# An attention backward kernel: column form instead of row form of V times dO for nine heads

## The chip, the cores and the metric

One core of one Trainium2 chip. The metric is device time in microseconds (us) of one execution. The kernel before takes 1744.86 us, the median of three runs (1738.73, 1744.86 and 1744.99).

## The reference, cut to what matters

The reference is one decode step of a transformer block with cached attention and a gated feed-forward part, and the gradients of its result towards ten of its inputs. There are B = 2 batch entries with H = 32 heads each, so 64 heads; each head has a cache K and a cache V of 8192 rows and 128 columns in bf16 (2 MB each). Per head, with one query row q and the gradient dO of the head's output o:

```python
p  = softmax(q @ K.T * Dh ** -0.5)     # 8192 numbers
o  = p @ V                              # 128 numbers
# backward
dV = outer(p, dO)                       # 8192 x 128, written out
dP = V @ dO                             # 8192 numbers: "V times dO"
dS = p * (dP - sum(o * dO))
dK = outer(dS, q) * Dh ** -0.5          # 8192 x 128, written out
```

Between the heads' forward and backward parts stands the rest of the block: `o` of all heads of a batch entry goes through `A_wo`, a layer norm and the feed-forward part, and the gradient comes back through the same to dO. This is one dependent chain for each batch entry: the first chain (b = 0) and the second chain (b = 1).

## The kernel before

The kernel is laid out in numbered **slots**. A head's forward job ("A") or backward job ("C") takes 8 slots for its transposes, one group of 8 blocks of 128 x 128 in each slot, and trails further work behind. `sC[n]` is the slot in which the backward job of head n begins. Within a slot, each engine runs its work in the order of the `PL_` numbers: EXP, T, X, S, B, MAX, TT, M, FREE, EV, DS, DK, TASK.[...]

Worked out from the code, with 64 heads, 8 groups a head and a chain of 40 slots (first) and 23 slots (second):

| what | slots |
|---|---|
| forward jobs of heads 0 to 38 | 0 to 312 |
| first chain | 272 to 312 |
| backward heads 0 to 24 alternate with forward heads 40 to 63 | 320 to 712 |
| `A_END`, the end of all forward work | 720 |
| backward heads 25 to 31, eight slots each | 712 to 768 |
| second chain | 721 to 744 |
| dO of batch entry 1, two heads for every two slots | 744 to 777 (the last is `t1`) |
| backward heads 62 and 63 (their V is kept from the forward part) | 768 to 784 |
| backward heads 32 to 61, with the weight gradients between them | 784 to the end |

The transposes of a group go to PSUM (`tp`, 3 buffers) and are copied to `kt` (4 buffers, shared with the chain's own transposes):

```python
def transposes(block, dve):
    tp = tps.tile([P, GRP, P], BF16, name="tp", tag="tp")
    for j in range(GRP):
        nc.tensor.transpose(tp[:, j, :], block(j), identb[:])        # L377
    kt = ktp.tile([P, GRP, P], BF16, name="kt", tag="kt")
    if dve:
        nc.vector.tensor_copy(kt[:], tp[:])                          # L380
    else:
        nc.scalar.copy(kt[:], tp[:])                                 # L382
    return kt

def c_t(n, g):                       # slot s + g
    if g == 0:
        if n in crow:
            nc.gpsimd.tensor_copy(qz[2 + n % 2][...], DO_bf[...])    # L1133
        else:
            DP[n] = head_ps()        # a PSUM bank of the two-buffer pool s_ps
    spare = A_END <= now[0] < t1 or now[0] >= max(sC) - 5 * NG
    kts[("c", n, g)] = transposes(..., g in (2, 6) and not spare)
    ...                              # after half of the groups: V's buffer is released
```

V times dO then has two forms. The **column form** takes each transposed block as weights and dO as one moving column, and leaves the result as a 128 x 64 tile; the **row form** takes dO (padded with zeros) as weights of 32 columns and streams four transposed blocks at once, in four column strips of the array, every second slot; its 128 x 512 result is copied by ScalarE and turned into columns by four fp32 matmuls (eight instructions in the trace):

```python
def c_s(n, g):                       # slot s + g + 2
    if n in crow:
        return s_rows(("c", n), n, g, c_bank)
    kt = kts.pop(("c", n, g))
    for j in range(GRP):             # column form, 8 x 8 = 64 a head
        nc.tensor.matmul(DP[n][:, cc:cc + 1], kt[:, j, :], DO_bf[:, b, h:h + 1], ...)   # L1164

def s_rows(key, i, g, bank):         # row form
    if g % SG < SG - 1:              # SG = 2: only after every second group
        return
    ...
    for j in range(NST):             # 4 x 4 = 16 a head
        nc.tensor.matmul(R_ps[key][NR * j:NR * (j + 1), :], w, kt[:, o:o + SW, :], ...)  # L410
    for k in range(SG):
        kts.pop(kt_of(g - k))

def rows_out(key):                   # slot s + 10
    nc.scalar.copy(t[:], R_ps.pop(key)[:])                           # L417, srow
def cols_out(ps, t):                 # slot s + 11, into a new head_ps()
    for c in range(SW):
        nc.tensor.matmul(sv[:, c, :], t[:, c * P:(c + 1) * P], ssel[:], ...)             # L430
```

The same helper serves the forward scores (L439 is their column form). dV and dK are made by VectorE (L1187) and sent from GpSimd (L1192, 1 MB each); their buffers `half` (21, of which weights and other data hold many during the chain) are the ones that V is loaded into (L187):

```python
x = 1 if n in crow else 0
at(s + 2 * q, PL_TT, ... c_dv(n, q))                        # q = 0..3
at(s + NG + LAG + 1 + (n in crow) + 2 * q, PL_DK, ... c_dk(n, q))
at(s + NG + LAG + x, PL_DS, ... c_ds(n))                    # dS from DP[n], L1208
```

The second chain's small results also lie in `s_ps`: `scr(n)` hands out columns 256 to 511 of the bank that `head_ps()` gave last, while a head uses columns 0 to 63.

Of the kernel before, what the change touches and what calls it, by code (L numbers as in the profile page):

```python
# [17 lines left out]
def kernel(  # L18
# [39 lines left out]
    NHD = B * H  # L58
# [4 lines left out]
    NG = KK // GRP  # L63
# [514 lines left out]
    def end_a(s):  # L578
        return s + MOFF + NG
# [462 lines left out]
    def lay(steps, slot):  # L1042
        for n, f in steps:
            at(slot, PL_TASK, f)
            slot += n
        return slot
# [15 lines left out]
    sC = []  # L1062
# [16 lines left out]
    R0 = min([sA[i] for i in byrows], default=sA[NHD - 1])  # L1079
    A_END = end_a(sA[NHD - 1]) + 1  # L1080
# [5 lines left out]
    t1 = lay(ch[1], CS1)  # L1086
# [53 lines left out]
            release()  # L1140
            pump()

    crow = {n for n in range(NHD) if R0 < sC[n] < max(sC) - 4 * NG}

    def c_bank():
        if now[0] <= A_END:
# [379 lines left out]
```

## Time and profile before

| | before |
|---|---|
| median of three runs | 1744.86 us |
| profiled span | 1742.8 us |
| PE (TensorE matmul) busy | 1454.8 us, 83% |
| DVE (VectorE) busy | 1150.7 us, 66% |
| ACT (ScalarE) busy | 1048.0 us, 60% |
| moved by DMA | 708.90 MB, mean 407 GB/s |

The page cuts the span into 40 slices and gives for each the busy share of every engine in tenths, the clock granted to TensorE, the DMA engines' busy share and the rate at which they moved data. The same can be asked for any stretch of the span. PE stands for the matmuls of TensorE, PEld for its weight loads, "issue" for idle time in which nothing that the profile shows was waited for.

### The profile page before, as it was taken

The page shows a single profiled execution, that of the slowest core. Times are in us where ns is not written, and L with a number is a line of the kernel's source. Part 1 is how long each engine was busy: PE and PEld are TensorE (multiplying, and loading weights), DVE is VectorE, ACT ScalarE, POOL GpSimd, SP SyncE. Part 2 cuts the span into 40 slices and gives each one's busy share as a digit, 9 for nine tenths or more (in the row PEclk, how much of TensorE's full clock was granted, in tenths as well). Part 3 has the DMA queues.
Part 4 walks back from the last instruction along what each step waited for, and adds up shares of the span by engine and source line. Part 5 has one row for each costly group of instructions (what it writes and reads, how often), then busy time and mean ns, then how long its engine had stood idle before and what let it go on. Part 6 is the DMA issues. An engine that isn't in the chain of part 4 may idle for free.

```text
span 1742.8 us, 48279 instructions
## 1 busy us (share of the span) xinstructions
PE 1454.8 (83%) x20723; PEld 1156.9 (66%) x20723; DVE 1150.7 (66%) x1575; ACT 1048.0 (60%) x1540; POOL 347.4 (20%) x730
## 2 busy tenths in 40 slices
PE   5999999989988788788788778887589797975784
PEld 5999998879766566666666666765355454554463
DVE  2666666857787667766666776675576566655676
ACT  4666666646566456555555555587456566655685
POOL 0334333312111111111111111111111111111111
PEclk7999999988998989898889988588655556568688
DMA  9999999999999999999999999999999999999998
GB/s 381 419 419 418 419 418 391 418 379 400 376 419 424 424 425 420 423 416 421 423 415 414 421 412 364 341 380 423 426 415 421 411 408 385 417 418 401 408 416 340
DMA packets 109378, 708.90 MB, mean 407 GB/s; under 512 B 11175, under 2 KB 17683, under 8 KB 27243
## 3 DMA queue, kind: packets, MB, share of 16 engines
q1 hardware_dynamic: 67280, 421.59, 59.6%
q0 software_dynamic: 36864, 268.45, 37.1%
q10 hardware_dynamic: 5019, 15.78, 2.3%
q8 instruction: 162, 2.65, 0.6%
q14 instruction: 53, 0.43, 0.1%
HBM read 421.57 MB, written 284.20 MB: 405 GB/s over the span
## 4 chain that ended last, share of the span: by engine, by line
DMA 33%; issue 27%; PE 27%; DVE 5%; POOL 4%; ACT 2%; SPq 1%; POOLq 0%; DVEq 0%; ACTq 0%
DMA half<-in_A_k_cache_dram 17%; DMA out_dram<-half 14%; PE tp L377 11%; PE m_ps L480 8%; POOL out_dram L1192 3%; DVE half L1187 2%; PE s_ps L439 2%; PE k_ps L502 2%; ACT kt L382 1%; PE m_ps L410 1%; DMA half<-in_w_mod_dram 1%; DVE ek L465 1%; PE s_ps L430 1%; DMA half<-in_A_wo_dram 1%; ACT srow L417 0%
## 5 line engine op out<-in xcount | busy, mean ns | idle before, releaser
L382 ACT COPY kt<-tp 128x1024 bf16<-128x1024 bf16 x794 | 797.3, 1020 | 594.8 <-PE tp L377 532.7
L377 PE MATMUL tp<-identb,half 128*128 128x128 bf16 x8192 | 724.2, 242 | 105.3 <-DMA half<-in_A_k_cache_dram 54.1
L377 PEld LDWEIGHTS <-half 128*128 128x128 bf16 x8192 | 579.5, 110 | 216.1 <-issue 149.3
L480 PE MATMUL m_ps<-ek,half 128*128 128x129 bf16 x4096 | 335.2, 225 | 6.8 <-DVE ek L465 3.2
L380 DVE COPY kt<-tp 128x1024 bf16<-128x1024 bf16 x230 | 158.4, 689 | 250.4 <-PE tp L377 250.2
L1192 POOL DMA_DIRECT2D out_dram<-half x256 | 136.2, 532 | 914.0 <-DVE half L1187 846.3
L480 PEld LDWEIGHTS <-half 128*128 128x128 bf16 x4096 | 257.2, 100 | 27.9 <-issue 27.8
L430 PE MATMUL s_ps<-ssel,srow 128*128 128x16 f32 x672 | 107.1, 294 | 50.0 <-ACT srow L417 49.7
L430 PEld LDWEIGHTS s_ps<-ssel,srow 128*128 128x128 f32 x672 | 100.1, 228 | 63.1 <-ACT srow L417 62.5
L439 PE MATMUL s_ps<-qT_bf,kt 128*128 128x1 bf16 x2496 | 107.5, 164 | 0.8 <-DVE lnst L1027 0.4
L439 PEld LDWEIGHTS <-kt 128*128 128x128 bf16 x2496 | 96.6, 97 | 1.4 <-issue 1.0
L1320 ACT CAST stg<-m_ps 128x512 bf16<-128x512 f32 (+2 forms) x124 | 72.5, 586 | 16.6 <-PE m_ps L1319 10.3
L1319 PE MATMUL m_ps<-half 2*128 2x512 bf16 (+2 forms) x124 | 70.2, 566 | 4.5 <-ACT half L1294 3.6
L502 PE MATMUL k_ps<-half,pz 128*32 128x512 bf16 x1024 | 68.0, 386 | 3.6 <-POOL pz L488 3.6
L451 DVE TENSOR_REDUCE nm<-s_ps 128x1 f32<-128x128 f32 x64 | 18.6, 291 | 35.2 <-PE s_ps L448 35.1
L502 PEld LDWEIGHTS <-pz 128*32 128x32 bf16 x1024 | 22.1, 96 | 25.0 <-POOL pz L488 5.6
L410 PE MATMUL k_ps<-kt,qz_109 128*32 128x512 bf16 x272 | 37.2, 531 | 0.2 <-ACT kt L382 0.2
L1319 PEld LDWEIGHTS <-half 2*128 2x128 bf16 (+1 forms) x124 | 12.7, 102 | 36.0 <-issue 31.2
L410 PE MATMUL k_ps<-kt,qz_110 128*32 128x512 bf16 x256 | 35.0, 537 | 0.0
L1402 ACT COPY kt<-tp 128x1024 bf16<-128x1024 bf16 x28 | 30.5, 1091 | 3.9 <-PE tp L1396 2.8
L417 ACT COPY srow<-m_ps 128x512 f32<-128x512 f32 x51 | 30.5, 597 | 0.0
L1294 ACT CAST half<-m_ps 2x512 bf16<-2x512 f32 (+1 forms) x36 | 20.3, 565 | 14.1 <-DMA out_dram<-half 12.4
(899 smaller groups left out, 1972.9 us busy)
## 6 DMA issues: line engine op xcount, KB each, us to landing
out_dram<-half POOLq DMA_DIRECT2D x256, 1024.0 KB, 13.9
half<-in_A_v_cache_dram SPq DMA_DIRECT2D x252, 1024.0 KB, 16.8
half<-in_A_k_cache_dram SPq DMA_DIRECT2D x128, 1024.0 KB, 19.6
out_dram<-stg ACTq DMA_DIRECT2D x22, 512.0 KB, 9.9
half<-in_A_wq_dram SPq DMA_DIRECT2D x8, 1024.0 KB, 11.0
half<-in_A_wo_dram SPq DMA_DIRECT2D x4, 1024.0 KB, 20.2
half<-in_w_mod_dram SPq DMA_DIRECT2D x3, 1024.0 KB, 16.7
half<-in_B_w_dram SPq DMA_DIRECT2D x3, 1024.0 KB
```

What stands on the lines that cost most here:

```text
L377: nc.tensor.transpose(tp[:, j, :], block(j), identb[:])
L380: nc.vector.tensor_copy(kt[:], tp[:])
L382: nc.scalar.copy(kt[:], tp[:])
L410: nc.tensor.matmul(R_ps[key][NR * j:NR * (j + 1), :], w, kt[:, o:o + SW, :], start=(a == 0), stop=(a == NSL - 1))
L430: nc.tensor.matmul(sv[:, c, :], t[:, c * P:(c + 1) * P], ssel[:], start=True, stop=True)
L439: nc.tensor.matmul(S_ps[i][:, cc:cc + 1], kt[:, j, :], qT_bf[:, h, b:b + 1], start=True, stop=True)
L480: nc.tensor.matmul(m[:, 0:P + 1], vb_(i, kk), t[:, kk % QK, 0:P + 1], start=(kk == 0), stop=(kk == KK - 1), skip_group_check=True)
L502: nc.tensor.matmul(kp["ps"][NR * j:NR * (j + 1), :], pz[:, o:o + NR], K[(i, kk // HK)][:, kk % HK:kk % HK + QP, :], start=False, stop=(h = ...
L1187: nc.vector.tensor_tensor(pair(t[:, o:o + QK, :]), QD[(n, which)][:].rearrange("p (a b) -> p a b", b=2).unsqueeze(1).to_broadcast((P, QK, ...
L1192: sq_.dma_start(src_of(dst, n)[:, hf * HK:(hf + 1) * HK, :], t[:])
L1319: nc.tensor.matmul(ps[:lw, 0:rw], rsl(ln, lc, lw, step), rsl(rn, rc, rw), start=True, stop=True)
L1320: nc.scalar.copy(st["t"][:lw, o:o + rw], ps[:lw, 0:rw])
```

## The change

The set `crow` names the heads whose backward job uses the row form. The change takes out of it the heads whose backward job begins from slot 712 (`A_END - NG`) to slot 777 (`t1`), that is, those that run beside the second chain and the dO of batch entry 1.

```diff
-    crow = {n for n in range(NHD) if R0 < sC[n] < max(sC) - 4 * NG}
+    crow = {n for n in range(NHD) if (R0 < sC[n] < A_END - NG or t1 < sC[n])
+            and sC[n] < max(sC) - 4 * NG}
```

With R0 = 312 and max(sC) = 1016, 59 heads were in the set and 50 remain. Heads 25 to 31, 62 and 63 leave it: nine heads. Nothing else in the kernel's text differs; all that follows from `n in crow` (the bank, the slots of dS and dK, the GpSimd copy of dO) goes with it. It is meant to relieve the stretch in which the second chain's own work on TensorE and ScalarE comes on top of the heads'.

## The prediction

> **What bounds the kernel now.** I read the page's 40 slices first. The kernel moves 708.90 MB, and in most slices the DMA engines are full at about 420 GB/s, so over most of its length the kernel is bound by its transfers, not by an engine.
>
> ```profile
> PEclk7999999988998989898889988588655556568688
> ...
> GB/s 381 419 419 418 419 418 391 418 379 400 376 419 424 424 425 420 423 416 421 423 415 414 421 412 364 341 380 423 426 415 421 411 408 385 417 418 401 408 416 340
> ```
>
> The rates show one dip in the middle: 364, 341 and 380 GB/s in slices 25 to 27. A slice is 43.6 us, so this is 1046 to 1176 us. Next I asked where the nine heads lie. The GpSimd copy L1133 marks each head's first slot, and the timeline has it at 1076.8 us (head 25), 1089.1, 1108.1, 1131.8, 1147.3, 1162.5, 1174.9 (head 31), 1188.3 and 1201.5 (heads 62 and 63); head 32 follows at 1225.6. So the changed heads sit in the dip and just after it. Stretches of 10 us there:
>
> ```profile
> core 0: us, PE busy (x) PEld busy (x) DVE busy (x) ACT busy (x) POOL busy (x), PEclk, DMA share, GB/s
> ...
> 1090.00:1100.00 10.00, 8.27 (x161) 7.37 (x161) 5.71 (x18) 2.65 (x4) 1.06 (x2) 0.54 0.97 370
> 1100.00:1110.00 10.00, 8.28 (x142) 6.89 (x141) 6.09 (x17) 6.90 (x12) 1.26 (x3) 0.50 0.81 323
> 1110.00:1120.00 10.00, 9.80 (x128) 9.20 (x127) 7.59 (x24) 5.36 (x6) 1.06 (x2) 0.50 0.88 293
> 1120.00:1130.00 10.00, 9.32 (x132) 7.91 (x131) 4.66 (x11) 6.87 (x10) 0.00 (x0) 0.50 0.94 356
> ...
> 1160.00:1170.00 10.00, 8.13 (x136) 6.83 (x133) 8.71 (x14) 9.84 (x12) 2.55 (x5) 1.00 1.01 392
> 1170.00:1180.00 10.00, 7.61 (x118) 6.23 (x115) 7.68 (x14) 9.95 (x15) 2.02 (x4) 0.98 1.01 423
> ```
>
> There are two different stretches. From 1090 to 1160 us TensorE is the bound: busy to 88% over these 70 us (61.24 us), at a granted clock down to 0.50, and the DMA engines are not full (share 0.93, 349 GB/s). From 1160 to 1205 us ScalarE is the bound among the engines (42.24 of 45 us), but the DMA engines are full again (1.01). After 1205 us VectorE even waits for output transfers to free buffers (11.6 us at once). So only time won before about 1160 us can shorten the kernel: it must let transfers run earlier that were idle then. What is won later lies beside full transfers.
>
> **What the Trainium skill says.** (1) "TensorEngine Tiling (Array Packing)", Key Properties: changing the tiling mode drains TensorE. The row form's matmuls use 32-column strips among full-width ones, so each batch should pay at both ends. The trace agrees: idle gaps of 0.20 us before and 0.43 us after on the weight loads, with no releaser.
>
> ```profile
> 1100.77 0.11 PEld L410 LDWEIGHTS <-qz_109 128*32 128x32 bf16 x4 [0.20 <-issue]
> 1100.77 0.62 PE L410 MATMUL k_ps<-kt,qz_109 128*32 128x512 bf16 x4
> 1101.32 0.10 PEld L1169 LDWEIGHTS <-Qr_bf 128*128 128x128 bf16 x1 [0.43 <-issue]
> ```
>
> (2) "TensorE: Matmul & The Clock Gate", Part 1: the array runs at half clock until it has been busy for a while, and drops back after an idle stretch. The trace has both levels here (0.50 and 1.00), and the fall comes at 1089 to 1092 us, where TensorE waits 2.49 us for the second chain. (3) "PSUM — Partial Sum Buffer", PSUM bank collisions: two engines may not touch one bank at once, so accesses have to be ordered by bank, not by address. The column form writes in the bank that also holds the chain's small results. The trace agrees that such waits exist: the forward column matmuls L439, which have nothing to do with the chain's data, waited 0.4 us for a VectorE read (L1027) and 0.3 us for a ScalarE read (L710).
>
> **The change part by part.** Removed for each of nine heads: 16 matmuls L410 in four batches, one ScalarE copy L417, eight fp32 matmuls L430 and one GpSimd copy. Added: 64 matmuls L1164, eight in a slot. The groups:
>
> ```profile
> L1164 PE MATMUL s_ps<-DO_bf,kt 128*128 128x1 bf16 x320 | 14.2, 165 | 3.7 <-ACT kt L382 2.5
> ...
> L417 ACT COPY srow<-k_ps 128x512 f32<-128x512 f32 x33 | 19.7, 598 | 11.6 <-DMA out_dram<-stg 9.9 <-ACT stg L1320 1.6
> ...
> L410 PE MATMUL k_ps<-kt,qz_109 128*32 128x512 bf16 x272 | 37.2, 531 | 0.2 <-ACT kt L382 0.2
> ```
>
> The mean of one matmul misleads, as they overlap; I take start to start from the timeline instead. From the lines above, a batch of four L410 at half clock costs 1101.32 - 1100.77 = 0.55 us. The group of transposes ahead of a batch is longer by the drain: 0.94 us (1112.57 to 1113.51) against 0.81 us where other full-width work follows (1114.54 to 1115.35). L430 lasts 1.71 us (1117.66 to 1119.37). The row form at half clock is thus 4 x (0.55 + 0.13) + 1.71 = 4.4 us a head. The column form does eight matmuls in 0.26 us at half clock (L1164, 1676.38 to 1676.64), so 8 x 0.26 = 2.1 us; beside another neighbour I saw 0.33 us, which would make 2.6. The saving is **about 2 us a head at half clock**. At full clock the same reading gives 4 x (0.34 + 0.08) + 0.91 = 2.6 us for the row form and 8 x 0.25 = 2.0 us for the column form:
>
> ```profile
> 1687.68 0.61 PE L377 MATMUL tp<-identb,half 128*128 128x128 bf16 x8
> 1688.13 0.34 PE L1164 MATMUL s_ps<-DO_bf,kt 128*128 128x1 bf16 x8
> 1688.38 0.61 PE L1396 MATMUL tp<-identb,half 128*128 128x128 bf16 x8
> ```
>
> The saving there is 0.6 us. Heads 26 and 27 run at half clock (2 x 2.1 = 4.2 us), heads 25 and 28 partly (I choose 1.3 each), head 29 mostly above (0.8): **about 7.5 us of TensorE before 1160 us**. Heads 30, 31, 62 and 63 save some 0.7 us each, 2.8 us, beside full transfers.
>
> ScalarE: nine copies of 0.6 us, 5.4 us, of which five heads' 3 us lie before 1160 us, where it isn't the bound. The row form also keeps a `kt` buffer a slot longer (the first of a pair is read three slots after it is made), with four buffers shared with the chain's transposes. That shows as ScalarE waiting for the row matmuls (1080 to 1205 us):
>
> ```profile
> ACT kt L382 <- PE tp L377: 12.7, 9, 5.1
> ACT kt L382 <- PE k_ps L410: 11.2, 9, 2.4
> ```
>
> Most of the 11.2 us must go, but TensorE is working meanwhile, so I count it inside the 7.5 us and not beside it. dS and dK come a slot earlier, and dK's VectorE work falls in odd slots instead of the even ones of dV, so output transfers leave singly and not in pairs; I give this no number.
>
> Against it stands the bank order. The chain's results are read by VectorE about 35 times in these slots, often behind a 1.22 us multiplication L1187, while TensorE has only a transposes' time of 0.45 to 0.85 us before the next column matmul into that bank. At a choice of 0.06 us each on average, 2 us.
>
> What comes out at the end: 7.5 - 2 = 5.5 us of the engines' path before 1160 us. How much unused transfer is there to be filled? From 1090 to 1160 us, (1 - 0.93) x 70 = 4.9 us by the share; by the rates of the seven stretches against 424 GB/s, 12.3 us. So I take some 4 us of the 5.5. The sum is 1744.9 - 4 = 1741 us, 0.2% less.
>
> **The rivals.** *Hidden altogether*: after 1160 us the transfers are full to nearly the end, and buffers limit loads before it as well (the load queue waited 125 us for output transfers between 1070 and 1230 us). If V's loads wait for output buffers and not for the transposes, the saved TensorE time changes nothing: 1744 to 1746 us. For it speaks this wait; against it the idle transfers just where TensorE is slowest. *The bank takes over*: if every column group waits for VectorE to finish a multiplication and then its read, 25 to 40 waits of up to 1 us come to TensorE, and the stretch gets longer by 10 us or more: some 1750 us. For it, VectorE is busy for 65% (1090 to 1160 us) to 79% (1160 to 1205 us) there; against it, the first chain ran in just this arrangement with waits of 0.7 us in all. *More than the sum*: without drains and waits on `kt`, TensorE may keep its full clock through the chain. If half of the 40 us at 0.50 ran at full clock, 10 us more would go, and all 12.3 us of transfer could be used: 1732 us. Against it, the chain's own waits (2.49 us for L840, 1.67 us for L894) stay and bring the clock down by themselves.
>
> **Range and chances.** The centre is 1741. The rivals' ends are 1732 and 1750; the three runs before already differ by 6 us. I set 1733 to 1748. Two per cent is 35 us, three times what the stretch has to give and more than the worst bank order could cost: 0.02, 0.96, 0.02.
>
> **What would show it.** L410 should fall by 144, L417 by 9, L430 by 72, and L1164 rise by 576. The nine heads' transposes should be done by some 5 to 8 us sooner. ScalarE's wait for `k_ps` L410 before 1205 us should go nearly to zero. The rates from 1090 to 1160 us should rise from 349 to about 370 GB/s, with no change of rate after 1225 us. A new wait of L1164 for VectorE reads (L797 to L806, L1003) over 3 us in sum would mean the bank order was underestimated; an unchanged rate beside faster TensorE would mean that buffers held the loads. I would be wrong altogether if the order of buffers shifted the later heads, which the change doesn't touch.

## The result, and the profile after

The changed kernel takes 1735.66 us (median of four runs) against 1744.92 us. The ratio of the runs is 0.9955 with a 95% interval of 0.9933 to 0.9977: about 8 us less, 4 to 12. Measured once more, in five executions beside 17 of the kernel before, the ratio was 0.9958 (0.9946 to 0.9970).

The page of the changed kernel, the rates in the 40 slices, now 43.3 us each:

```profile
GB/s 383 418 419 418 419 419 389 418 384 403 376 420 424 425 425 421 425 417 413 425 419 414 423 421 358 397 423 424 422 396 425 415 419 376 420 415 397 387 421 349
```

The dip is still there in slice 25 (358 GB/s), but slices 26 and 27 have gone from 341 and 380 to 397 and 423. Stretches of 10 us of the changed kernel (length; busy time and count of TensorE's matmuls, of its weight loads, of VectorE, ScalarE and GpSimd; clock; DMA share; GB/s):

```profile
1090.00:1100.00 10.00, 8.99 (x191) 8.75 (x189) 7.63 (x22) 5.86 (x7) 1.59 (x3) 0.50 1.00 374
1100.00:1110.00 10.00, 9.79 (x218) 9.79 (x218) 8.51 (x26) 5.08 (x10) 1.03 (x2) 0.50 1.01 415
1110.00:1120.00 10.00, 9.28 (x196) 8.70 (x195) 7.22 (x17) 9.67 (x14) 1.62 (x4) 0.84 1.01 410
1120.00:1130.00 10.00, 9.17 (x172) 8.68 (x169) 7.54 (x12) 9.96 (x12) 1.06 (x2) 0.79 1.01 416
...
1160.00:1170.00 10.00, 8.11 (x178) 7.60 (x174) 8.58 (x17) 9.84 (x14) 1.60 (x4) 1.00 1.01 419
```

From 1100 us on the transfers run at over 400 GB/s, where before they fell to 293. Over the whole 70 us from 1090 to 1160 us it is 412 GB/s against 349.

How far the engines came is read from dS (L1208 before, L1209 after), one instruction a head. The timeline has head 24's, which the change doesn't touch, and head 62's, eight heads later. Before, and then after:

```profile
1081.38 0.35 DVE L1208 SCALAR_TENSOR_TENSOR ds_20879<-s_ps,SIG,e_20552 128x128 bf16<-128x128 f32 x1
...
1207.62 0.34 DVE L1208 SCALAR_TENSOR_TENSOR ds_23107<-s_ps,SIG,e_22681 128x128 bf16<-128x128 f32 x1
```

```profile
1079.21 0.34 DVE L1209 SCALAR_TENSOR_TENSOR ds_20890<-s_ps,SIG,e_20552 128x128 bf16<-128x128 f32 x1
...
1189.79 0.35 DVE L1209 SCALAR_TENSOR_TENSOR ds_23379<-s_ps,SIG,e_22944 128x128 bf16<-128x128 f32 x1
```

That is 126.2 us before and 110.6 us after. Some 1.8 us of the difference (one slot: 110.6 us for 63 slots) is only that dS stands a slot earlier in the column form; the engines gained about 14 us. They don't keep it all. Head 32 has the row form in both kernels; its dS, before and then after:

```profile
1238.25 0.35 DVE L1208 SCALAR_TENSOR_TENSOR ds_23293<-s_ps,SIG,e_22913 128x128 bf16<-128x128 f32 x1
```

```profile
1228.40 0.34 DVE L1209 SCALAR_TENSOR_TENSOR ds_23631<-s_ps,SIG,e_23216 128x128 bf16<-128x128 f32 x1
```

It comes 156.9 us after head 24's before, and 149.2 us after: 7.7 us are left, which is about what the whole kernel gains. From there to the end the two take the same, 504.6 and 504.8 us. Where the other 6 us go is seen in the longest waits of the changed kernel from 1190 to 1240 us:

```profile
DVE half L1188 <- DMA out_dram<-half: 27.0, 3, 17.3
...
PE s_ps L1165 <- DVE kt L380: 14.3, 1, 14.3
```

VectorE stands for 17.3 us at once until an output transfer frees a buffer, and TensorE 14.3 us behind it. Before, the longest such wait of VectorE was 11.6 us. What the engines win beyond the transfers, they give back here.

The rest of the forecast counts are there in the groups of the changed kernel:

```profile
L1165 PE MATMUL s_ps<-DO_bf,kt 128*128 128x1 bf16 x896 | 39.8, 165 | 23.8 <-DVE kt L380 14.3 <-DVE O_276 L1253 1.9 <-ACT kt L382 1.8
...
L417 ACT COPY srow<-k_ps 128x512 f32<-128x512 f32 x25 | 14.8, 593 | 9.2 <-DMA out_dram<-stg 7.5 <-ACT stg L1321 1.6
```

L1165 is the column form (320 before, 896 now, 576 more); the ScalarE copies are 25 and 50 instead of 33 and 51, nine less; L410 falls from 1344 to 1200 and L430 from 672 to 600, as forecast. ScalarE's wait for L410, 11.2 us before, is gone from the waits between 1080 and 1205 us. And the order by bank shows as five waits of the column matmuls in that window, 6.4 us in sum:

```profile
PE s_ps L1165 <- DVE O_276 L1253: 1.9, 1, 1.9
PE s_ps L1165 <- DVE rtot L828: 1.7, 1, 1.7
...
PE s_ps L1165 <- DVE SIG L806: 1.5, 1, 1.5
...
PE s_ps L1165 <- DVE prod L800: 0.9, 1, 0.9
...
PE s_ps L1165 <- DVE lnst L1027: 0.4, 1, 0.4
```

### The profile page after: what moved, and what is told of

Its sections match the earlier page's. It is cut to its first block, busy times and chain, and to the rows that moved or that the text cites. A ratio compares the mean times of both kernels' runs of the same rounds, so it can differ in the third digit from the quotient of the medians.

```text
span 1733.2 us, 48977 instructions
## 1 busy us (share of the span) xinstructions
PE 1450.6 (84%) x21083; PEld 1162.7 (67%) x21083; DVE 1150.6 (66%) x1575; ACT 1043.9 (60%) x1531; POOL 342.5 (20%) x721
## 4 chain that ended last, share of the span: by engine, by line
DMA 32%; PE 31%; issue 26%; DVE 4%; POOL 3%; ACT 3%; SPq 1%; POOLq 0%; ACTq 0%; DVEq 0%
DMA out_dram<-half 15%; DMA half<-in_A_k_cache_dram 15%; PE tp L377 13%; PE m_ps L480 9%; POOL out_dram L1193 3%; PE s_ps L439 2%; PE k_ps L502 2%; PE m_ps L410 2%; DVE half L1188 2%; ACT kt L382 2%; PE s_ps L430 1%; DMA half<-in_w_mod_dram 1%; DVE ek L465 1%; DMA half<-in_A_wo_dram 1%; ACT srow L417 0%
## 5 line engine op out<-in xcount | busy, mean ns | idle before, releaser
L430 PE MATMUL s_ps<-ssel,srow 128*128 128x16 f32 x600 | 96.0, 294 | 44.0 <-ACT srow L417 43.8
L430 PEld LDWEIGHTS s_ps<-ssel,srow 128*128 128x128 f32 x600 | 89.7, 229 | 56.7 <-ACT srow L417 56.2
L439 PEld LDWEIGHTS <-kt 128*128 128x128 bf16 x2496 | 96.8, 97 | 1.6 <-issue 1.0
L1165 PE MATMUL s_ps<-DO_bf,kt 128*128 128x1 bf16 x896 | 39.8, 165 | 23.8 <-DVE kt L380 14.3
L1165 PEld LDWEIGHTS <-kt 128*128 128x128 bf16 x896 | 36.8, 101 | 27.9 <-DVE kt L380 14.5
L410 PE MATMUL k_ps<-kt,qz_109 128*32 128x512 bf16 x208 | 30.1, 569 | 0.0
```

Source lines behind the costliest of these rows:

```text
L439: nc.tensor.matmul(S_ps[i][:, cc:cc + 1], kt[:, j, :], qT_bf[:, h, b:b + 1], start=True, stop=True)
```

## The experiments

Three theories of where the gain comes from were set against each other. **TensorE time**: the row form's strips, drains and conversion, less the column matmuls. **The `kt` buffers**: the row form holds them a slot longer. **The slots of dS and dK**: they come a slot earlier, and dK's multiplications fall in odd slots. Each experiment puts one of them back into the changed kernel, or brings one of them to the kernel before.

Beside the ratio I give two readings of the profiled execution: the *path*, from head 24's dS to head 62's (which comes one slot, about 1.8 us, earlier where head 62 has the column form's slots), and the *lost transfer*, the time that would carry what the DMA engines moved less than 424 GB/s in the 130 us after head 24's dS. The path ends at head 62, so head 63 is not in it. Two executions of the changed kernel agree in it to 0.3 us, but at head 31 they still stood 2.3 us apart (96.6 and 98.9 us after head 24's dS). Single executions of one kernel lay up to 13 us apart in their whole time, so the ratio with its interval is the measure of the total, and the two readings only say what happened in the stretch.

| kernel | ratio to before (95%) | path us | lost transfer us |
|---|---|---|---|
| before | 1 | 126.2 | 13.7 |
| changed | 0.9955 (0.9933 to 0.9977) | 110.6 | 3.1 |
| changed, again | 0.9958 (0.9946 to 0.9970) | 110.9 | 4.5 |
| first four heads only | 0.9959 (0.9944 to 0.9975) | 118.0 | 6.0 |
| last five heads only | 0.9999 (0.9989 to 1.0009) | 119.5 | 10.9 |
| changed, `kt` held longer | 0.9973 (0.9964 to 0.9982) | 110.8 | 4.5 |
| changed, strips added | 0.9981 (0.9971 to 0.9990) | 112.2 | 4.3 |
| changed, conversion added | 0.9977 (0.9968 to 0.9986) | 120.1 | 7.5 |
| changed, dS and dK late (even) | 0.9985 (0.9977 to 0.9993) | 116.8 | 7.0 |
| changed, dK late (odd) | 0.9966 (0.9952 to 0.9980) | 114.4 | 7.0 |
| changed, own banks | 0.9967 (0.9955 to 0.9979) | 111.8 | 3.8 |
| before, row form without hold | 1.0005 (0.9995 to 1.0016) | 126.3 | 13.0 |
| before, dK late (odd) | 0.9980 (0.9968 to 0.9992) | 116.1 | 8.0 |
| changed, all row heads' dK odd | 0.9947 (0.9933 to 0.9960) | 110.7 | 3.8 |

**The changed kernel again**, for a reference on the same chip as several others. No edit.

> The changed kernel once more, unaltered, so that it is measured on the same chip and in the same rounds as the runs beside it: 0.995 to 0.997 of the kernel before.

Measured: 0.9958, as before.

**Which heads count: the first four, the last five.**

```diff
-    crow = {n ... if (R0 < sC[n] < A_END - NG or t1 < sC[n]) ...
+    crow = {n ... if (R0 < sC[n] < A_END - NG or A_END + 3 * NG <= sC[n]) ...   # heads 25 to 28 column
+    crow = {n ... if (R0 < sC[n] < A_END + 3 * NG or t1 < sC[n]) ...            # the other five column
```

> Column form for heads 25 to 28 only (slots 712 to 743); heads 29 to 31, 62 and 63 keep the row form. If only time won before about 1160 us counts, because transfers are full afterwards, this run keeps nearly the whole gain: 1736 to 1738 us. If each head is worth the same share of the 9.3 us wherever it runs, four of nine heads bring 4.1 us: 1741 us. The transfer rate from 1090 to 1150 us should be over 400 GB/s in the first case.

> Column form for heads 29 to 31, 62 and 63 only; heads 25 to 28 keep the row form. If only time won before about 1160 us counts: 1743 to 1745 us, the engines ahead by some 5 us at 1200 us and nothing of it left after 1230 us. If each head counts the same: five of nine, 1740 us.

Measured: 0.9959 and 0.9999. The first four heads bring 7.1 us, all of the gain within the interval; the last five bring nothing (0.2 us, between 1.9 us gained and 1.6 us lost). The engines gained in both: 8.2 us of path in the first, 6.8 us in the second (1.8 us of it the earlier slot). At head 32's dS the first is still 5.6 us ahead of the kernel before, the second 1.8 us. The stretch from 1090 to 1160 us, first of the four heads' run, then of the five heads':

```profile
1090.00:1160.00 70.00, 60.67 (x1196) 56.10 (x1194) 57.77 (x124) 58.24 (x76) 11.91 (x22) 0.82 0.97 393
```

```profile
1090.00:1160.00 70.00, 59.30 (x931) 51.44 (x932) 47.64 (x110) 49.11 (x67) 8.71 (x18) 0.73 0.96 367
```

393 and 367 GB/s against 349 before (from 1090 to 1150 us the four heads' run had 388, not the 400 expected): path that is won where transfers were idle shortens the kernel, path won where they were full doesn't.

**The `kt` buffers: held longer in the changed kernel, released at once in the row form.**

```diff
+        if n in nine and g % 2 == 0:
+            return                       # an even group's matmuls run with the odd group's
+        for g in ((g - 1, g) if n in nine else (g,)):
```

> The changed kernel, but in the nine heads the eight column matmuls of every even group are put off by one slot and run with those of the odd group, so that their kt buffer is held as long as in the row form; no work is added. If the gain comes from the earlier release of kt buffers: back to 1741 to 1745 us, with ScalarE waiting some 10 us for the column matmuls. If it comes from the TensorE time of the row form (drains, strips and conversion): 1735 to 1737 us.

The other way round, in the kernel before, the row form reads each group in its own slot:

```diff
+        if n in nine:
+            kt = kts.pop(("c", n, g))
+            for j in (0, 1) if g % SG == 0 else (2, 3):
+                nc.tensor.matmul(R_ps[("c", n)][NR * j:NR * (j + 1), :], ..., kt[:, o:o + SW, :], ...)
+            return
```

> The kernel before, but in the nine heads the row form runs two of its strips in every slot instead of four in every second one, so that no kt buffer is held for a third slot; the same 16 matmuls in eight batches, so twice as many mode switches, and the conversion stays. Theory of kt buffers: most of the gain comes although TensorE has more to do, 1737 to 1740 us. Theory of TensorE time: no gain or a loss, 1745 to 1750 us.

Measured: 0.9973 and 1.0005. With the longer hold, the waits of ScalarE between 1080 and 1205 us have a line again (L1169 is the column matmul of that kernel):

```profile
ACT kt L382 <- PE s_ps L1169: 4.9, 4, 2.1
```

That is less than the 10 us expected and the 11.2 us of the row form, so the test is a partial one. The path is the same 110.8 us and the lost transfer 4.5 us. Without the hold, the row form has no such wait and gains nothing, with a path of 126.3 us. (Its eight batches a head change the array's mode twice as often, and its strips wait 4.6 us for ScalarE's copy L417, which the kernel before doesn't show, so that run alone would not settle it.) The hold is not what makes the path longer. The median with the longer hold is 2 to 3 us over the changed kernel's, with overlapping intervals; the stretch doesn't show where.

**TensorE time: strips, conversion.** The strips of the row form are added to the column form, reading the group at hand, result unused:

```diff
+        if n in nine and g % 2 == 1:
+            for j in range(NST):
+                nc.tensor.matmul(R_ps["x"][NR * j:NR * (j + 1), :], qz[...], kt[:, o:o + SW, :], ...)
```

> The changed kernel with the 16 strip matmuls of the row form added back for the nine heads (four batches a head, on the block group at hand, result not used), so TensorE pays the mode switches and the streaming again, but without a longer hold of kt and without the conversion. Theory of TensorE time: a batch costs 0.42 us at full and 0.68 us at half clock, 1.7 to 2.7 us a head, some 11 us for the first five heads, of which most returns: 1741 to 1744 us. Theory of kt buffers: 1736 us or a little more, as the release is unchanged.

The conversion, also with its result unused:

```diff
+        if n in nine and g == NG - 1:    # one matmul fills the bank
+            nc.tensor.matmul(R_ps["x"][:], identb[:], kt[:, 0:SW, :], start=True, stop=True)
...
+            at(s + NG + LAG, PL_EXP, nine_rows)        # ScalarE copy, L417
+            at(s + NG + LAG + 1, PL_EXP, nine_cols)    # eight fp32 matmuls, L430
```

> The changed kernel with the conversion of the row form added back for the nine heads: one 128 x 512 ScalarE copy and eight fp32 matmuls a head (and one full-width matmul that fills the bank copied), result not used. Theory of TensorE time: 0.9 us at full to 1.7 us at half clock a head plus the wait for the copy, some 6 us before 1160 us: 1739 to 1741 us. Theory of kt buffers: 1736 us, at most 1737.

Measured: 0.9981 and 0.9977, medians of 1738.63 us (between what the two theories expected) and 1739.38 us (as TensorE time expected). They differ in the stretch. The strips lengthen the path by 1.5 us for nine heads, far from the 11 us expected for five, and the transfers stay full:

```profile
1090.00:1160.00 70.00, 62.36 (x1282) 54.41 (x1282) 54.49 (x120) 55.86 (x76) 9.57 (x18) 0.85 1.01 405
```

The conversion lengthens it by 9.4 us and takes the transfers down:

```profile
1090.00:1160.00 70.00, 62.99 (x1133) 61.22 (x1135) 51.92 (x115) 52.45 (x72) 9.57 (x18) 0.68 0.98 385
```

So the conversion carries the TensorE part of the path. The totals don't tell the two apart: with the strips as with the conversion the kernel takes 3 to 4 us more than the changed one (the strips' interval just fails to overlap that of the changed kernel's second measurement, the conversion's does overlap). With the strips the profiled stretch doesn't show those microseconds, and with the conversion most of the path's loss is made up by head 32, whose dS comes 150.2 us after head 24's, where the changed kernel has 149.2 and 148.8. Where the totals' 3 to 4 us go stays open.

**The slots of dS and dK.** In the changed kernel the nine heads get the row form's slots back:

```diff
-            at(s + NG + LAG + 1 + (n in crow) + 2 * q, PL_DK, ...)
+            at(s + NG + LAG + 1 + (n in crow or n in nine) + 2 * q, PL_DK, ...)
-        at(s + NG + LAG + x, PL_DS, ...)
+        at(s + NG + LAG + (n in crow or n in nine), PL_DS, ...)
```

> The changed kernel, but in the nine heads dS and the four steps of dK keep the slots of the row form (one slot later, even slots, beside the steps of dV). If the earlier, spread output transfers matter: 1739 us or more. If only TensorE time or the kt buffers matter: 1735 to 1737 us.

Then dK later still, in odd slots, first in the changed kernel (`2 if n in nine else n in crow`), then in the kernel before (`(n in crow) + (n in nine)`):

> The changed kernel, but in the nine heads the steps of dK start two slots later than there, one later than in the row form, in odd slots again; dS keeps its early slot. If the late dK of the earlier run cost time because two VectorE multiplications then stand in one slot ahead of the chain's small reads (TensorE waited 6.1 us for the read of SIG there): no such wait, and the time of the changed kernel. If it cost time because output transfers start later: as slow as with the late dK or slower, 2 to 5 us over the changed kernel.

> The kernel before (row form for all), but in the nine heads the steps of dK start one slot later, in odd slots, so that VectorE has one multiplication in each slot instead of two in every second. If this pairing is part of the gain by itself: 2 to 4 us below the kernel before. If the row form's TensorE work holds the stretch anyway, or if early output transfers are what counts: no gain, or 1 to 2 us lost.

Measured: 0.9985, 0.9966 and 0.9980, medians of 1739.57, 1738.10 and 1740.07 us: the first and the third as expected if the slots count, the second 1.9 us over the changed kernel of the same rounds, between its two expectations. The late even dK gives back more than half of the gain, with this line among TensorE's waits (L1166 is the column matmul there):

```profile
PE s_ps L1166 <- DVE SIG L806: 6.1, 7, 0.9
```

In odd slots that wait is gone, and the total is lower although dK comes later (0.9966 against 0.9985; the intervals just overlap). The path is 2.4 us shorter, but 1.8 us of that is the slot by which dS is earlier again, and the lost transfer is the same 7.0 us. Against the changed kernel this run's path is still 3.5 to 3.8 us longer, while its total isn't clearly so: a later dK seems to cost something besides the pairing, and what, stays open. The clearest run is the third: the row form stays whole, nine heads' dK only moves to a *later* slot, and the kernel gains 3.5 us (1.4 to 5.6), the path 10.1 us. (The path's gain isn't kept: at head 32's dS it is 10.0 us, but from there to the end this execution took 508.3 us, the one before 504.6. Why, no run shows.) The timelines show what happens in the stretch. Of the kernel before, VectorE and TensorE beside the second chain:

```profile
1110.76 1.22 DVE L1187 TENSOR_TENSOR half<-DOr,e_21256 128x2048 bf16<-128x2048 bf16 x1
...
1111.90 1.22 DVE L1187 TENSOR_TENSOR half<-Qr,ds_21132 128x2048 bf16<-128x2048 bf16 x1
...
1113.03 0.69 DVE L780 COPY kt<-tp 128x1024 bf16<-128x1024 bf16 x1
...
1113.51 0.62 PE L410 MATMUL k_ps<-kt,qz_109 128*32 128x512 bf16 x4
...
1114.33 0.35 PE L793 MATMUL s_ps<-d_attn_bf,kt 128*128 128x1 bf16 x8 [0.20 <-DVE ffn L940]
...
1117.20 0.16 DVE L806 COPY SIG<-s_ps 128x4 f32<-128x4 f32 x1
```

And of the row form with the late odd dK:

```profile
1110.41 1.22 DVE L1188 TENSOR_TENSOR half<-DOr,e 128x2048 bf16<-128x2048 bf16 x1
...
1111.55 0.68 DVE L780 COPY kt<-tp 128x1024 bf16<-128x1024 bf16 x1
...
1113.16 0.62 PE L410 MATMUL k_ps<-kt,qz 128*32 128x512 bf16 x4
...
1113.71 0.37 PE L793 MATMUL s_ps<-d_attn_bf,kt 128*128 128x1 bf16 x8
...
1115.97 0.16 DVE L806 COPY SIG<-s_ps 128x4 f32<-128x4 f32 x1 [0.34 <-PE s_ps L805]
```

In even slots, two multiplications of 1.22 us (dV and dK) stand in VectorE's queue ahead of the chain's copy and its small operations, and the timeline has them run in that order, the program's. In odd slots it is one: from the start of the multiplication to the chain's copy it is 1111.55 - 1110.41 = 1.14 us, where it was 1113.03 - 1110.76 = 2.27 us. TensorE's chain matmuls L793 no longer wait for the operations behind it: they follow the strips by 0.55 us instead of 0.82. From the start of that multiplication to the chain's read of SIG it is 5.56 us instead of 6.44.

**The order by bank.**

```diff
+            elif n in nine and A_END <= now[0] < t1 - 2:
+                DP[n] = mtps() if n % 2 else c_bank()   # not the bank of the chain's results
```

> The changed kernel with the column results of heads 26 to 31 and 62 in PSUM banks of their own instead of the bank that holds the chain's small results. If the order by bank is what makes the column matmuls wait for VectorE (6.4 us in sum between 1080 and 1205 us in the changed kernel), those waits shrink to 2 us or less and the engines reach head 32 some 2 to 4 us sooner. As the transfers are full from 1090 us on in the changed kernel, the total should stay within 1 us of it; a fall of 2 us or more would mean that engine time still counts there.

Measured: 0.9967, a path of 111.8 us and a lost transfer of 3.8 us, both as in the changed kernel. Of the column matmuls' five waits for VectorE from 1080 to 1205 us one is left (L1168), below a wait that the changed kernel had at only 0.6 us:

```profile
PE s_ps L840 <- DVE O_bf L831: 2.5, 1, 2.5
PE s_ps L1168 <- DVE O L1256: 1.7, 1, 1.7
```

TensorE now waits 2.5 us for the chain itself: the wait for the bank had stood in place of another. The engines did not come further, and neither did the total.

**Odd slots for all row heads**, the version that these runs point to:

```diff
-            at(s + NG + LAG + 1 + (n in crow) + 2 * q, PL_DK, ...)
+            at(s + NG + LAG + 1 + 2 * (n in crow) + 2 * q, PL_DK, ...)
```

> The changed kernel, and in all 50 heads that keep the row form the steps of dK start one slot later, in odd slots, as the run with the kernel before and late odd dK suggested (it gained 3.5 us with nine heads). If spreading VectorE's multiplications over all slots helps wherever the row form runs: 2 to 6 us below the changed kernel, 1730 to 1734 us. If it helps only where the engines and not the transfers are the bound, and most of these heads run beside full transfers: within 1.5 us of the changed kernel, 1735 to 1738 us.

Measured: 1734.43 us, ratio 0.9947 (0.9933 to 0.9960). That is the lowest median of all kernels here, but its interval overlaps those of the changed kernel (0.9955 and 0.9958), and the difference of medians to the rerun is 1.8 us, between the two expectations. It beats the kernel before; that it beats the changed one isn't shown.

## Why the prediction was right or wrong

The time, 1735.7 us, lies in the range of 1733 to 1748 us, and no comparison came near 2%. The mechanism at the end of the chain was right: transfers bound the kernel, they were idle from 1090 to 1160 us, and only time won there counts. The first four heads bring the whole gain, the last five none, and what the engines win beyond that goes into a wait of 17.3 us for output transfers. The gain itself was twice the forecast, about 8 us for 4.

**The step that failed** is the reading "From 1090 to 1160 us TensorE is the bound", on which the gain was priced in TensorE time alone. With TensorE's work left whole, moving dK's VectorE work by one slot shortened the path by 10.1 us. What it mis-sized is the sum "7.5 - 2 = 5.5 us of the engines' path before 1160 us". For all nine heads the prediction had 7.5 + 2.8 = 10.3 us less 2 us; the path, up to head 62, measured about 14 us. Term by term:

- *"dK's VectorE work falls in odd slots ... I give this no number"* was the term left out. By itself, in the row form, the odd slots shortened the path by 10.1 us and the kernel by 3.5 us; taken back from the changed kernel they cost 6.2 us of path, about 4.4 beyond the slot that dS moves, and some 5 us in all. The prediction looked for the effect in the transfers; in the row form it is VectorE's queue, in which the chain's small operations wait. In the changed kernel part of it is left open, as dK two slots later cost path in odd slots too.
- *The strips with their drains*, 4 x 0.68 us a head at half clock, were priced as if TensorE never had slack. Added back, they cost 1.5 us of path, though the total rose by 3 to 4 us in a place that isn't found.
- *The conversion*, 1.71 us a head at half and 0.91 us at full clock, sums to about 10 us for nine heads by the prediction's clocks, and cost 9.4 us when added back (with its copy, and one matmul to fill the bank).
- *The `kt` hold* was rightly not counted apart: the wait went, and where 4.9 us of it were put back, the path didn't move.
- *The order by bank*, 2 us by choice: the waits summed to 6.4 us, but with banks of their own for seven of the nine heads the path was no shorter. No cost is shown. The sign set for an underestimate, over 3 us of waits, was met only with lines beyond those that it named (which have 2.4 us), and it was no measure of the cost.

The terms don't add. Conversion and slots together exceed the 14 us, perhaps because each delays the same slots and the longest of several waits sets a slot; no run tests this. I can't split the gain into shares.

**The step from path to time** took "some 4 us of the 5.5", and named two measures of idle transfer: 4.9 us by share and 12.3 us by rate. The rate was the one to trust: the lost transfer fell by 9 to 11 us, twice what the share had offered, and 7.7 us of the engines' lead were left at head 32. At a share of 0.93 the engines carried 349 of 424 GB/s, which is 0.82.

**The rivals.** "Hidden altogether" holds for the last five heads only. "The bank takes over" did not happen. "More than the sum" was nearest in size, and the clock from 1090 to 1160 us did rise, from 0.63 to 0.78. It is not shown as a cause: the row form without hold had 0.78 as well and gained nothing, and the changed kernel with dK late in odd slots had 0.71 and gained 5.9 us. It isn't ruled out as a part either: the row form with odd slots had 0.78 too, and whether a shorter queue raised the clock or ran beside it, no run separates.

## What to carry to other kernels

When a dependent chain runs beside bulk work, look at the order of each engine's instructions, slot by slot: two long operations in one slot and none in the next cost 10.1 us of path here, more than 16 strip matmuls a head on TensorE (1.5 us). Price a change only where the stretch's bound lies, and there count idle transfer by its rate, not by its busy share. Then follow the lead past the stretch: of 14 us won there, 7.7 were left at the next unchanged head. And give an effect a number, however rough, before leaving it out: a term without one is a term set to zero.

## What was not expected of the hardware

Sixteen more strip matmuls a head, with their changes of mode, lengthened the path by 1.5 us in all, though gaps of 0.20 and 0.43 us stand around such a batch at half clock in the trace; the 3 to 4 us that the whole kernel lost with them are not found there. And a moved wait is not a saved one: 6.4 us of waits for a PSUM bank could be taken away without shortening anything.
